# Linear attention and two MLPs on one core: sums of weight parts and low halves of W2's parts made by GpSimd in place of VectorE

## The chip, the cores and the metric

The kernel runs on one core of a Trainium2 chip. The metric is the time of one execution in microseconds on the device, as the median of several runs. A profile is one more execution, taken by the hardware profiler; its own time stands beside it. Engines are named PE (TensorE, matmuls), PEld (TensorE's weight loads), DVE (VectorE), ACT (ScalarE), POOL (GpSimd) and SP (SyncE, whose queue issues DMAs).

## The reference

```python
kv = np.einsum('bhsd,bhse->bhde', k, v)          # 4 x 8 heads, 576 tokens, 64 wide
out = np.einsum('bhsd,bhde->bhse', q, kv)
rms = np.sqrt(np.mean(out * out, axis=-1, keepdims=True) + 1e-06)
x = (out / rms * g_norm)                         # -> [2304, 512]
h = x @ moe_w_in                                 # [512, 2048]
g = np.maximum(h, 0.0) + np.log1p(np.exp(-np.abs(h)))
x = (g @ moe_w_out)                              # [2048, 512]
h = x @ moe2_w_in
g = np.maximum(0.01 * h, h)
return (g @ moe2_w_out)
```

The weights arrive as 64-bit floats.

## The kernel before

The attention takes the first 80 us. After it the activations lie in SBUF as `xy`, 512 features by 2304 tokens, and the two MLPs run over them in place. Each MLP is cut into four groups of 512 hidden columns (`NG` = 4, so groups 0 to 7), each group into three tiles of 768 tokens (`NTP`), each tile into two steps of 256 hidden columns.

A matmul in full precision is three matmuls here. An operand is split into a high half, which ScalarE makes by a copy to the narrower type fp32r, and a low half, the rest, which is one subtraction of VectorE with two inputs in SBUF; the products high by high, high by low and low by high are added in PSUM. Line 850 and line 855 do this for the hidden activations `g` (in `parts`), lines 739 and 734 for the inputs, lines 1003 and 1006 for W2's parts.

To save matmuls, most products of 2 x 2 blocks are made from seven products of sums of blocks in place of eight (`PROD` names the sums). So weights and activations are first added and subtracted blockwise. `split_pair` does that for W1: four sums in series of 128x256 (line 656), then the two halves of the seven parts (lines 673 and 677). It is called twice for each of the eight groups; for the first group with `first` set, during the attention. `w2_part` does it for W2 in the groups 1, 2, 5, 6 and 7 (`SG`): over its seven calls four sums of 128x512 (line 989) and for each part one high half (line 1003) and one low half (line 1006). Those seven calls stand in the last tile before such a group: this document calls that the entry into the group. Before both, `decode_w` turns 64-bit weights into 32-bit ones: a copy on ScalarE (line 595), then a shift (line 601) and two operations with two inputs in SBUF (lines 607 and 613) on VectorE.

What comes out of a step's products lies in PSUM banks. ScalarE copies some of it out (line 1119), VectorE adds the rest (line 1126), and the bank is free for a later product (line 821). The second layer's results are added to `xy` by VectorE from PSUM (lines 1050 and 711). In these two kinds of addition only one input lies in SBUF.

The order is made by `Plan`, when the program is built. Each piece of work is given by `op` with an engine or a choice of engines, a cost in microseconds (`t_d` for VectorE, `t_a` for ScalarE, `t_p` for GpSimd), what it reads and what it writes. `Plan.run` goes through time with one clock for each engine, takes for an engine that is free the ready piece with the earliest due time, and writes the instructions in that order into each engine's queue. The order is fixed then: an instruction that waits holds up all that stands behind it in its queue. The engines' clocks in the plan are independent of each other.

Of the kernel before, what the change touches and what calls it, by code (L numbers as in the profile page):

```python
# [19 lines left out]
class Plan:  # L20
# [18 lines left out]
    def op(self, cost, fn, reads=(), writes=(), due=None):  # L39
        o = {"cost": cost, "fn": fn, "succ": [], "n": len(self.ops)}  # L40
        deps = {}
        for k in reads:
            if k in self.writer:
                deps[self.writer[k]["n"]] = self.writer[k]
        for k in writes:
            for d in [self.writer.get(k), *self.readers.get(k, ())]:
                if d is not None:
                    deps[d["n"]] = d
        for k in reads:
            self.readers.setdefault(k, []).append(o)  # L50
        for k in writes:
            self.writer[k], self.readers[k] = o, []
        o["deps"] = list(deps.values())
        for d in o["deps"]:
            d["succ"].append(o)
        o["due"] = self.pe
        if "PE" in cost:
            self.pe += cost["PE"]
        else:
            o["due"] += self.AHEAD  # L60
        if due is not None:
            o["due"] = due
        self.ops.append(o)
        return o
# [67 lines left out]
def linear_attention_two_mlps(  # L132
# [32 lines left out]
    nc = tc.nc  # L165
    B, H, S, D = q.shape
    NT, DM = out.shape
    DFF = w1.shape[1] // 2
    P = 128
# [166 lines left out]
    op = plan.op  # L336
    ENG = {"D": nc.vector, "P": nc.gpsimd}

    def t_a(n):
        return 0.1 + n * 0.84e-3  # L340

    def t_d(n, fast=False):
        return 0.08 + n * (0.8e-3 if fast else 1.04e-3)

    def t_p(n):
        return 0.2 + n * 2.5e-3
# [301 lines left out]
    def part(r, j, n=1):  # L648
        return r.keys(1024 * j, 1024 * (j + n))

    def split_pair(i, u, first=False):
        r, w_ = sraw[i], wst[u]

        def combine(j, a, b, sign):
            def fn(e):
                ENG[e].tensor_tensor(r[:, j, :], r[:, a, :], r[:, b, :], sign)

            op({"D": t_d(256)}, fn, part(r, a) + part(r, b), part(r, j))

        def parts(j, at, n):  # L660
            hk = w_.keys(at * 1024, (at + n) * 1024)
            lk = w_.keys(7168 + at * 1024, 7168 + (at + n) * 1024)
            sk = part(r, j, n)
            m = n * 256

            def ends(a):
                return (
                    w_[:, a, at * 256:(at + n) * 256],
                    r.ap.rearrange("p a b -> p (a b)")[:, j * 256:(j + n) * 256],
                )  # L670

            def hi(e):
                nc.scalar.activation(*ends(0), AF.Copy)

            def lo(e):
                out, in_ = ends(1)
                ENG[e].tensor_tensor(out, in_, ends(0)[0].bitcast(F32), ALU.subtract)

            op({"A": t_a(m)}, hi, sk, hk)
            op({"D": t_d(m)}, lo, sk + hk, lk)  # L680


        if first:
            x_, hk = wx[u], wx[u].keys()
            op({"A": t_a(256)}, lambda e: nc.scalar.activation(x_[:, 0, :], r[:, 0, :], AF.Copy),
               part(r, 0), hk)
            op(
                {"D": t_d(256)},
                lambda e: nc.vector.tensor_tensor(
                    x_[:, 1, :], r[:, 0, :], x_[:, 0, :].bitcast(F32), ALU.subtract  # L690
                ), part(r, 0) + hk, hk,
            )
        parts(1, 0, 3)
        combine(1, 0, 1, ALU.add)
        combine(0, 2, 0, ALU.subtract)
        combine(2, 1, 2, ALU.subtract)
        combine(3, 3, 2, ALU.subtract)
        parts(0, 3, 4)
# [273 lines left out]
    def w2_part(g, i):  # L972


        def blk(a, u):
            at = (3 + 4 * u) * KI // 4
            ap = bufs["rc"][:, at:at + 2 * DM].rearrange("p (m f) -> p m f", m=2)
            return ap[:, :, a * 256:(a + 1) * 256]

        def bk(a, u):  # L980
            return [k_ for m in range(2) for k_ in fS[u][m].keys(1024 * a, 1024 * (a + 1))]

        r = [(lambda a=a, u=u: blk(a, u), bk(a, u)) for a in range(2) for u in range(2)]
        r.append((lambda: fT.ap, fT.keys()))

        def combine(to, x, y, sign):
            op(
                {"D": t_d(512)},
                lambda e: nc.vector.tensor_tensor(r[to][0](), r[x][0](), r[y][0](), sign),
                r[x][1] + r[y][1], r[to][1],  # L990
            )

        if i == 1:
            combine(4, 0, 1, ALU.add)
        elif i == 2:
            combine(0, 2, 0, ALU.subtract)
            combine(2, 4, 2, ALU.subtract)
        elif i == 3:
            combine(4, 3, 2, ALU.subtract)
        src, sk = r[(2, 4, 2, 4, 0, 3, 1)[i]]  # L1000
        w_ = wS[g // NG][PROD[i][2]]
        hk, lk = w_.keys(0, 2048), w_.keys(2048)
        op({"A": t_a(512)}, lambda e: nc.scalar.activation(w_[:, 0], src(), AF.Copy), sk, hk)  # L1003
        op(
            {"D": t_d(512)},
            lambda e: nc.vector.tensor_tensor(  # L1006
                w_[:, 1], src(), w_[:, 0].bitcast(F32), ALU.subtract
            ), sk + hk, lk,
        )
# [17 lines left out]
    def second(t):  # L1027
# [26 lines left out]
        def piece(i, j):  # L1054
# [48 lines left out]
            if t % NTP == NTP - 1 and g + 1 in SG:  # L1103
                w2_part(g + 1, i)
# [175 lines left out]
    for s in range(2 * NT2 + 2):  # L1280
# [11 lines left out]
        if enters:  # L1292
            g_held[0] = True
            for i in range(2):
                g_part(t, i)
                w2_part(t // NTP, i)
# [26 lines left out]
        if enters:  # L1323
            g_part(t, 3)
            for i in range(2, 7):
                w2_part(t // NTP, i)
# [62 lines left out]
```

## Time and profile before

| | us |
|---|---|
| median of 3 runs | 801.38 |
| the three runs | 800.7, 801.38, 802.01 |
| the profiled execution, whole | 800.57 |
| its span, first to last instruction | 798.5 |
| PE busy | 787.5 |
| DVE busy | 688.2 |
| ACT busy | 453.3 |
| POOL busy | 18.2 |

The span is what the profile's rows cover; 2.07 us of the profiled execution lie outside it. Matmuls follow each other in a pipeline, so PE's busy time tells that it had work, not that the array was full; how often PE waited, and for whom, is told by the view of waits. An idle time of another engine matters only where PE waits for that engine.

### The profile page before, as it was taken

Reading aid. Unit: us, or ns where it says so; the run is one execution under the profiler, and the core shown is the slowest. Engines: PE = TensorE matmul, PEld = TensorE weight load, DVE = VectorE, ACT = ScalarE, POOL = GpSimd, SP = SyncE. Lnnn points to the kernel's source line nnn. Section 1 sums busy time; section 2 is a strip of 40 time slices with the busy share of each in tenths; the row PEclk is TensorE's granted clock in tenths of the full one; section 3 lists DMA queues with packets and bytes.
Section 4 is the critical chain, followed back from the end, with each engine's and each line's share of the span. In section 5 each row is a group of like instructions: output and inputs, shape, how many; then the busy total and the mean of one; then the engine's idle time right before and its main releaser. Section 6 shows DMA issues by size and latency. Waiting matters only on the chain.

```text
span 798.5 us, 13018 instructions
## 1 busy us (share of the span) xinstructions
PE 787.5 (99%) x4962; PEld 774.9 (97%) x4962; DVE 688.2 (86%) x1129; ACT 453.3 (57%) x753; POOL 18.2 (2%) x35
## 2 busy tenths in 40 slices
PE   8899999999999999999999999999999999999997
PEld 7899999999999999999999988989999999999997
DVE  6989997989999999996698877868989999997776
ACT  5877965565465455563466566546456555554341
POOL 3320000000000000000000000000000000000000
PEclk9999999999999999999999999999999999999999
DMA  9990993675874675596776986874854764753914
GB/s 311 306 332 27 361 369 127 273 286 188 308 259 148 226 303 182 224 336 213 289 289 265 376 300 241 307 229 179 326 170 145 281 233 184 255 195 122 317 40 119
DMA packets 77294, 192.47 MB, mean 241 GB/s; under 512 B 11569, under 2 KB 50481, under 8 KB 77233
## 3 DMA queue, kind: packets, MB, share of 16 engines
q1 hardware_dynamic: 75344, 190.73, 66.4%
q10 hardware_dynamic: 1888, 0.92, 0.4%
q8 instruction: 39, 0.64, 0.3%
q14 instruction: 23, 0.18, 0.1%
HBM read 152.31 MB, written 39.32 MB: 240 GB/s over the span
## 4 chain that ended last, share of the span: by engine, by line
PE 97%; ACT 1%; DMA 1%; DVE 1%; SPq 0%; issue 0%; POOL 0%; ACTq 0%; POOLq 0%
PE ps L821 42%; PE ps L1072 17%; PE ps L1172 13%; PE ps L1077 11%; PE ps L1190 6%; PE ps L459 2%; PE ps L915 2%; PE ps L422 2%; PE ps L414 1%; PE ps L543 1%; DMA qa<-in_q_dram 1%; PE ps L465 0%; PE ps L425 0%; PE ps L555 0%; ACT xy L531 0%
## 5 line engine op out<-in xcount | busy, mean ns | idle before, releaser
L821 PE MATMUL ps<-ra 128*128 128x384 f32 x1932 | 387.4, 335 | 0.0
L821 PEld LDWEIGHTS ps<-ra 128*128 128x128 f32 x1932 | 334.9, 188 | 3.8
L850 ACT ACTIVATE rb<-mf 128x768 fp32r<-128x768 f32 x131 | 110.8, 846 | 91.9 <-PE ps L1072 43.9
L1072 PE MATMUL ps<-rb 128*128 128x256 f32 x1134 | 153.1, 281 | 0.0
L1072 PEld LDWEIGHTS ps<-rb 128*128 128x128 f32 x1134 | 148.7, 189 | 0.0
L855 DVE TENSOR_TENSOR rb<-mf,rb 128x768 fp32r<-128x768 f32 x131 | 124.6, 953 | 16.0 <-ACT rb L850 15.5
L1050 DVE TENSOR_TENSOR xy<-ps,xy 128x512 f32<-128x512 f32 (+2 forms) x213 | 116.3, 549 | 23.2 <-PE ps L1072 16.1
L1172 PE MATMUL ps<-rb 128*128 128x384 f32 x576 | 113.7, 334 | 0.0
L1172 PEld LDWEIGHTS ps<-rb 128*128 128x128 f32 x576 | 101.1, 188 | 0.0
L1077 PE MATMUL ps<-rb 128*128 128x384 f32 x504 | 100.8, 334 | 0.0
L1119 ACT ACTIVATE mf<-ps 128x384 f32<-128x384 f32 x118 | 57.8, 490 | 72.6 <-PE ps L821 69.8
L1126 DVE TENSOR_TENSOR mf<-ps,mf 128x384 f32<-128x384 f32 x118 | 65.4, 554 | 36.6 <-PE ps L821 35.1
L1077 PEld LDWEIGHTS ps<-rb 128*128 128x128 f32 x504 | 88.5, 188 | 0.0
L1190 PE MATMUL ps<-rb 128*128 128x512 f32 x216 | 56.8, 394 | 0.0
L836 ACT ACTIVATE mf<-mf 128x768 f32<-128x768 f32 (+1 forms) x44 | 29.9, 679 | 27.9 <-DVE mf L1126 27.9
L1190 PEld LDWEIGHTS ps<-rb 128*128 128x128 f32 x216 | 39.9, 188 | 5.7
L952 DVE TENSOR_TENSOR mf<-mf 128x768 f32<-128x768 f32 x40 | 38.1, 953 | 0.8 <-ACT mf L842 0.3
L842 ACT ACTIVATE mf<-mf 128x384 f32<-128x384 f32 (+1 forms) x42 | 27.6, 658 | 18.9 <-DVE mf L1126 18.5
L1006 DVE TENSOR_TENSOR rb<-rc,rb 128x512 fp32r<-128x512 f32 x35 | 23.8, 685 | 2.0 <-ACT rb L1003 2.0
L1003 ACT ACTIVATE rb<-rc 128x512 fp32r<-128x512 f32 x35 | 21.5, 626 | 5.7 <-PE ps L1190 2.4
L607 DVE SCALAR_TENSOR_TENSOR sqr<-mf,sqr 128x512 int32<-128x512 int32 x35 | 24.0, 685 | 0.3
L706 ACT ACTIVATE xy<-ps 128x512 f32<-128x512 f32 (+1 forms) x26 | 14.2, 548 | 14.6 <-PE ps L1172 11.6
(117 smaller groups left out, 775.3 us busy)
## 6 DMA issues: line engine op xcount, KB each, us to landing
ra<-xscr SPq DMA_DIRECT2D x131, 768.0 KB, 6.3
xscr<-ra SPq DMA_DIRECT2D x30, 768.0 KB, 6.3
mf<-in_moe_w_in_dram SPq DMA_DIRECT2D x18, 512.0 KB, 5.1
xscr<-rc SPq DMA_DIRECT2D x12, 768.0 KB, 3.9
mf<-in_moe_w_out_dram SPq DMA_DIRECT2D x17, 512.0 KB, 5.0
lf<-in_moe_w_out_dram SPq DMA_DIRECT2D x15, 512.0 KB, 4.3
lf<-in_moe_w_in_dram SPq DMA_DIRECT2D x14, 512.0 KB, 5.3
qa<-in_q_dram SPq DMA_DIRECT2D x16, 256.0 KB, 5.5
```

The source lines that it names most:

```text
L821: nc.tensor.matmul(o, w_[:, a, c:c + P], e_[:, b, kk, :], start=(not on and kk == 0 and n == 0), stop=(kk == 1 and n == 2), skip_group_che ...
L836: {"A": t_a(n)}, lambda e: nc.scalar.activation(dst(), src(), AF.Softplus),
L850: {"A": t_a(n)}, lambda e: nc.scalar.activation(g[:, 0, :, :], c.ap, AF.Copy),
L855: lambda e: nc.vector.tensor_tensor(g[:, 1, :, :], c.ap, g[:, 0, :, :].bitcast(F32), ALU.subtract),
L952: lambda e: nc.vector.tensor_tensor(to.ap, x.ap, y.ap, ALU.subtract),
L1050: {"D": t_d(n)}, lambda e: nc.vector.tensor_tensor(dst, src, dst, ALU.add),
L1072: nc.tensor.matmul(y[:, 256 * (j % 2):256 * (j % 2 + 1)], G_[:, a, m, js], w_[:, b, m, :], **flags)
L1077: nc.tensor.matmul(y[:, :BN], w_[:, a, m, js], G_[:, b, m, :], **flags)
L1119: {"A": t_a(BN)}, lambda e: nc.scalar.activation(c[:, m, :], src, AF.Copy),
L1126: lambda e: nc.vector.tensor_tensor(c[:, m, :], src, c[:, m, :], ALU.add),
L1172: nc.tensor.matmul(y[:, :BN], w_[m][:, a, js], G_[:, b, m, :], start=(u == 0 and m == 0 and i == 0), stop=(u == 1 and m == 1 and i == 2),)
L1190: nc.tensor.matmul(y, G_[:, a, m, js], w_[m][:, b, :], start=(u == 0 and m == 0 and i == 0), stop=(u == 1 and m == 1 and i == 2),)
```

## The change

Three kinds of work get GpSimd as their engine, with GpSimd's cost in the plan: the sums of W1 parts in `split_pair`, except those of the first group; the sums of W2 parts in `w2_part`; and the low halves of W2's seven parts there.

```diff
@@ -655,7 +655,7 @@
             def fn(e):
                 ENG[e].tensor_tensor(r[:, j, :], r[:, a, :], r[:, b, :], sign)
 
-            op({"D": t_d(256)}, fn, part(r, a) + part(r, b), part(r, j))
+            op({"D": t_d(256)} if first else {"P": t_p(256)}, fn, part(r, a) + part(r, b), part(r, j))
 
         def parts(j, at, n):
             hk = w_.keys(at * 1024, (at + n) * 1024)
@@ -985,8 +985,8 @@
 
         def combine(to, x, y, sign):
             op(
-                {"D": t_d(512)},
-                lambda e: nc.vector.tensor_tensor(r[to][0](), r[x][0](), r[y][0](), sign),
+                {"P": t_p(512)},
+                lambda e: nc.gpsimd.tensor_tensor(r[to][0](), r[x][0](), r[y][0](), sign),
                 r[x][1] + r[y][1], r[to][1],
             )
 
@@ -1002,8 +1002,8 @@
         hk, lk = w_.keys(0, 2048), w_.keys(2048)
         op({"A": t_a(512)}, lambda e: nc.scalar.activation(w_[:, 0], src(), AF.Copy), sk, hk)
         op(
-            {"D": t_d(512)},
-            lambda e: nc.vector.tensor_tensor(
+            {"P": t_p(512)},
+            lambda e: nc.gpsimd.tensor_tensor(
                 w_[:, 1], src(), w_[:, 0].bitcast(F32), ALU.subtract
             ), sk + hk, lk,
         )
```

In the plan `t_d(256)` is 0.35 us, `t_d(512)` 0.61, `t_p(256)` 0.84 and `t_p(512)` 1.48. The plan makes a new order from them. The order of PE's instructions is the same in both kernels. GpSimd's queue, which ended with the attention, gets 111 instructions behind it.

VectorE's queue at the entry into group 1, before, from the low half of an activation (line 855) to the second of the two additions from PSUM (line 1126; `ps_84` is the bank):

```order
L855 TENSOR_TENSOR rb<-mf,rb 128x768
L613 SCALAR_TENSOR_TENSOR rc<-rc,sqr 128x512
L952 TENSOR_TENSOR mf<-mf 128x768
L989 TENSOR_TENSOR rc<-rc 128x512
L989 TENSOR_TENSOR rc<-rc 128x2x256
L855 TENSOR_TENSOR rb<-mf,rb 128x768
L1006 TENSOR_TENSOR rb<-rc,rb 128x512
L1126 TENSOR_TENSOR mf<-ps_85,mf 128x384
L989 TENSOR_TENSOR rc<-rc 128x2x256
L989 TENSOR_TENSOR rc<-rc 128x512
L1006 TENSOR_TENSOR rb<-rc,rb 128x512 x2
L1126 TENSOR_TENSOR mf<-ps_84,mf 128x384
```

The same stretch of VectorE's queue now:

```order
L855 TENSOR_TENSOR rb<-mf,rb 128x768
L952 TENSOR_TENSOR mf<-mf 128x768
L855 TENSOR_TENSOR rb<-mf,rb 128x768
L601 TENSOR_SCALAR sqr<-lf 128x512
L1126 TENSOR_TENSOR mf<-ps_85,mf 128x384
L607 SCALAR_TENSOR_TENSOR sqr<-mf,sqr 128x512
L613 SCALAR_TENSOR_TENSOR lf<-lf,sqr 128x512
L601 TENSOR_SCALAR sqr<-lf 128x512
L607 SCALAR_TENSOR_TENSOR sqr<-lf,sqr 128x512
L1126 TENSOR_TENSOR mf<-ps_84,mf 128x384
```

Four sums and three low halves have left it, and five decode operations (lines 601, 607 and 613) that stood further back have taken their places.

GpSimd's queue now, from the end of the attention (line 360) through the entry into group 1 to the first sum of the entry into group 2:

```order
L360 TENSOR_SCALAR kp_121<-ka_102 128x512
L656 TENSOR_TENSOR lf<-lf 128x256 x4
L656 TENSOR_TENSOR mf<-mf 128x256 x4
L1006 TENSOR_TENSOR rb<-rc,rb 128x512
L989 TENSOR_TENSOR rc<-rc 128x512
L989 TENSOR_TENSOR rc<-rc 128x2x256
L1006 TENSOR_TENSOR rb<-rc,rb 128x512
L989 TENSOR_TENSOR rc<-rc 128x2x256
L989 TENSOR_TENSOR rc<-rc 128x512
L1006 TENSOR_TENSOR rb<-rc,rb 128x512 x5
L989 TENSOR_TENSOR rc<-rc 128x512
```

Before, its queue ended with the first of these rows; the others were VectorE's.

## Rows read from the trace of the kernel before

**Rows 1.** The page: busy times by engine, and the chain that ended last.
```profile
PE 787.5 (99%) x4962; PEld 774.9 (97%) x4962; DVE 688.2 (86%) x1129; ACT 453.3 (57%) x753; POOL 18.2 (2%) x35
...
PE 97%; ACT 1%; DMA 1%; DVE 1%; SPq 0%; issue 0%; POOL 0%; ACTq 0%; POOLq 0%
```

**Rows 2.** Waits of PE, first and last of seven: us in total, times, longest.
```profile
PE ps L1241 <- POOL ident masks.py:199: 2.0, 1, 2.0
...
PE ps L555 <- ACT xy L531: 0.3, 1, 0.3
```

**Rows 3.** Timeline of DVE, first sums that move: start, duration, line, operation, count.
```profile
133.47 1.80 DVE L656 TENSOR_TENSOR lf<-lf 128x256 f32<-128x256 f32 x4
```

**Rows 4.** The five entries: length, busy PE, PEld, DVE, ACT, POOL, granted clock, DMA.
```profile
161.90:183.90 22.00, 22.00 (x129) 22.00 (x128) 20.69 (x33) 14.57 (x27) 0.00 (x0) 1.00 0.85 312
251.20:272.50 21.30, 21.30 (x125) 21.30 (x124) 20.66 (x35) 13.24 (x24) 0.00 (x0) 1.00 0.73 259
485.80:545.20 59.40, 59.40 (x302) 53.66 (x301) 42.83 (x67) 34.45 (x58) 0.00 (x0) 1.00 0.71 252
614.80:633.80 19.00, 19.00 (x137) 19.00 (x137) 18.38 (x31) 11.34 (x19) 0.00 (x0) 1.00 0.80 284
704.30:723.40 19.10, 19.10 (x137) 19.10 (x136) 19.02 (x32) 11.97 (x20) 0.00 (x0) 1.00 0.81 287
```

**Rows 5.** DVE by line and shape: count, busy us, mean ns, idle before.
```profile
L855 DVE TENSOR_TENSOR rb<-mf,rb 128x768 fp32r<-128x768 f32 x131 | 124.6, 953 | 16.0 <-ACT rb L850 15.5
L1126 DVE TENSOR_TENSOR mf<-ps,mf 128x384 f32<-128x384 f32 x118 | 65.4, 554 | 36.6 <-PE ps L821 35.1 <-issue 0.3
...
L607 DVE SCALAR_TENSOR_TENSOR sqr<-mf,sqr 128x512 int32<-128x512 int32 x35 | 24.0, 685 | 0.3
L1006 DVE TENSOR_TENSOR rb<-rc,rb 128x512 fp32r<-128x512 f32 x35 | 23.8, 685 | 2.0 <-ACT rb L1003 2.0
...
L656 DVE TENSOR_TENSOR mf<-mf 128x256 f32<-128x256 f32 x36 | 15.3, 424 | 0.8
...
L601 DVE TENSOR_SCALAR sqr<-mf 128x512 int32<-128x512 int32 x22 | 9.3, 421 | 4.9 <-ACT mf L595 4.5
...
L510 DVE SCALAR_TENSOR_TENSOR fm<-fm,fa 128x20 f32<-128x20 f32 x8 | 1.8, 221 | 0.3
```

**Rows 6.** Timeline of DVE, the last low halves that move.
```profile
722.09 1.29 DVE L1006 TENSOR_TENSOR rb<-rc,rb 128x512 fp32r<-128x512 f32 x2
```

**Rows 7.** Timeline of POOL and DVE in the attention, two meetings.
```profile
15.23 1.23 DVE L677 TENSOR_TENSOR ra<-mf,ra 128x1024 fp32r<-128x1024 f32 x1
...
15.90 1.03 POOL L360 TENSOR_SCALAR kp<-ka 128x512 f32<-128x512 f32 x1 [1.41 <-DMA ka<-in_k_dram]
...
27.00 0.62 POOL L360 TENSOR_SCALAR qp<-qa 128x512 f32<-128x512 f32 x1 [1.00 <-DMA qa<-in_q_dram]
...
27.12 0.52 DVE L510 SCALAR_TENSOR_TENSOR fm<-fm,fa 128x20 f32<-128x20 f32 x1
```

**Rows 8.** Timeline of DVE at the entry into group 1.
```profile
165.76 0.95 DVE L855 TENSOR_TENSOR rb<-mf,rb 128x768 fp32r<-128x768 f32 x1
166.63 0.69 DVE L613 SCALAR_TENSOR_TENSOR rc<-rc,sqr 128x512 int32<-128x512 int32 x1
...
168.10 1.41 DVE L989 TENSOR_TENSOR rc<-rc 128x512 f32<-128x512 f32 x2
...
170.30 0.69 DVE L1006 TENSOR_TENSOR rb<-rc,rb 128x512 fp32r<-128x512 f32 x1
...
171.49 1.41 DVE L989 TENSOR_TENSOR rc<-rc 128x512 f32<-128x512 f32 x2
173.81 1.29 DVE L1006 TENSOR_TENSOR rb<-rc,rb 128x512 fp32r<-128x512 f32 x2 [0.91 <-ACT rb L1003]
175.02 0.55 DVE L1126 TENSOR_TENSOR mf<-ps,mf 128x384 f32<-128x384 f32 x1
```

**Rows 9.** Timeline of PE, the product that takes up the freed bank.
```profile
177.05 1.20 PE L821 MATMUL ps<-ra 128*128 128x384 f32 x6
```

## The prediction

> **What bounds the kernel now.** I began with the page's busy times and its chain: TensorE is busy 787.5 us of a span of 798.5 us, and 97% of the chain that ended last is TensorE's own work [rows 1]. The second view is who TensorE waited for. It has seven rows that sum to 6.5 us, and all of them are lines of the warm-up and the attention, its transposes and small matmuls [rows 2]; the attention is over before 80 us. The first sum that the change moves stands at 133.47 us [rows 3]. From there to the end TensorE waits for nobody: in the five stretches in which W2's parts are made it is busy for the whole of each, at a granted clock of 1.00, its upper level of 2.4 GHz [rows 4]. So the time is the attention's start plus an unbroken run of matmuls, in an order that the change leaves as it was. Nothing on VectorE can shorten that run; it can only be broken. The question is whether VectorE, 19.02 us busy of 19.10 in the tightest of these stretches [rows 4], comes late for TensorE after the change.
>
> **What is removed.** 56 of the 64 sums of W1 parts leave VectorE (the first pair's eight stay) and all 20 sums and 35 low halves of W2 parts: 56 x 0.423 + 55 x 0.685 = 61.4 us of VectorE [rows 5]. I count that as worth nothing: it is cover, not path. A gain is excluded for the same reason, since none of TensorE's seven waits lies behind the first moved instruction. Behind the last matmul too nothing changes: the last moved low halves stand at 722.09 us [rows 6], 76 us ahead of the end.
>
> **What is added.** GpSimd gets 111 subtractions and additions with two inputs in SBUF. It has none in this trace; the nearest row is its copy of 128x512 with one input, 0.62 us where nothing is in its way [rows 7]. If the second input were free, a W2 operation would take 0.62 us; if the inputs are read one behind the other, twice that, 1.24 us; with the write as a third pass, 0.14 + 3 x 0.48 = 1.58 us, where 0.48 us is the part that works on the data, read off just below, and 0.14 us the start. I take 1.24 us: two inputs and one engine that took 0.62 us for one. The Trainium skill (GPSIMD Engine Reference, section 3.1) gives 4497 ns for such an addition of 2048 columns; a quarter is 1.12 us, an estimate, by which the sum below would come to 805.4 us in place of 807.8.
>
> **The port.** Rows 7 show what the two engines do to each other. At 15.90 us GpSimd's copy meets a VectorE subtraction with two SBUF inputs that runs from 15.23 to 16.46: it takes 1.03 us in place of 0.62 and ends at 16.93, 0.47 us behind VectorE's end. At 27.00 us it is the other way about: GpSimd runs from 27.00 to 27.62, and VectorE's small operation on two SBUF tensors, line 510, which starts at 27.12, takes 0.52 us, against a mean of 221 ns over its line [rows 5], and ends at 27.64, with GpSimd. So an operation of VectorE with two SBUF inputs and one of GpSimd don't run side by side: whoever has begun keeps the other out. From the first meeting a GpSimd operation needs about 0.48 us of its 0.62 alone. A W2 operation of 1.24 us would then keep VectorE's two-input work out for 1.1 us. What was 0.685 us on VectorE becomes up to 1.1 us of VectorE standing still. The Trainium skill says the same in its page SBUF — State Buffer (section "SBUF: two separate sides"): VectorE's second port is GpSimd's only one, an exclusive lock for a whole instruction. The trace agrees, with the two meetings above; without such a lock the change would cost nothing.
>
> **Where it breaks.** The planner counts GpSimd as free beside VectorE and fills VectorE's emptied places with other work. The first entry into a group with W2 parts shows it, from the low half at 165.76 us to the addition of line 1126 that ends at 175.57 us, 9.81 us [rows 8]. In the changed order the same two ends have other rows between them. Gone are four sums (2 x 1.41 us), three low halves (0.69 and 1.29), and line 613 of 0.69, which now stands earlier; idle in it were 0.91 us. That leaves 9.81 - 0.91 - 2.82 - 1.98 - 0.69 = 3.4 us. Come in have five decode rows (lines 601, 607, 613, 601, 607), 2 x 0.421 + 3 x 0.685 = 2.9 us [rows 5]. VectorE's own work is 6.3 us. Seven GpSimd operations belong to the same stretch. If each meets a two-input operation, they add 7 x 1.1 = 7.7 us: 14.0 us, 4.2 later than before. If two of the seven fall beside the additions from PSUM or the shifts, it is 5 x 1.1 = 5.5: 11.8 us, 2.0 later. TensorE takes up the bank that this addition frees at 177.05 us [rows 9], a lead of 1.48 us. So TensorE stands still for 0.5 to 2.7 us there; I take the middle, 1.6.
>
> There are five such entries. In four of them VectorE has 0.1 to 1.3 us of idle time in some 20 us; in the one at 485.8 us it has 16.6 us, and that one I count at nothing [rows 4]. The sum is 4 x 1.6 = 6.4 us. The W1 sums come in 14 rows of four: 4 holds of about 0.55 us (half a W2 hold) in place of 4 x 0.42, a slip of 0.5 us, under the lead of 1.48 us: nothing, and 14 x 0.5 = 7 us if that lead is used up already. What is queued behind GpSimd's results: ScalarE's copies of line 1003 to the high halves and, on VectorE, line 677. Ahead of them in the order stands what the planner reckons GpSimd to need, 1.48 and 0.84 us, over my prices, so they wait only as far as the port makes GpSimd late.
>
> The profiled execution took 800.57 us (span 798.5 and 2.07 around it): 800.57 + 6.4 = 807.0. It lies 0.81 us under the median of the runs, 801.38, so the forecast is **807.8 us**, 0.8% slower.
>
> **The rivals.** First, **no change**. It decides at the number of meetings: 9.81 + 1.48 - 6.3 = 5.0 us is room for four holds of 1.1 us of the seven. If the operations mostly fall beside work that reads PSUM, where the trace shows 0.62 us and no delay, each entry stays under the lead. Time 801.4 us, within about 0.6. For it speaks that 61.4 us leave VectorE; against it that of the ten rows that VectorE keeps in the stretch worked out six have two SBUF inputs and two are shifts, of which no row shows whether they meet GpSimd.
>
> Second, **a dearer GpSimd**. At 1.58 us a hold is 1.44 us: 7 holds give 5.1 us an entry, 5 give 2.2, in the middle 3.65, four entries 14.6 us: 816 us, at most 821.8. The sums then also come late for ScalarE, whose copies from PSUM stand behind line 1003, and the W1 rows begin to tell. For it speaks that no row shows a two-input operation on GpSimd; against it that its one-input copies are steady at 0.62.
>
> Third, **faster**: only if something in the 76 us behind 722 us or in the attention moves, and the order shows no moved row there.
>
> **How the numbers follow.** The forecast gets 0.58, the dearer GpSimd 0.21, no change 0.18, faster 0.03. A measurement of this kernel can tell 0.2%, 1.6 us, from nothing. The forecast at its low end, 4 x 0.5 = 2.0 us, is still slower by more than that, so slower has 0.58 + 0.21 + a little of the second case's edge, 0.80, the same 0.17 and faster 0.03. The range runs from 801.3 us, in the middle of the no-change case, to 818 us, inside the dearer case: some 0.12 lie below and 0.07 above.
>
> **What would show it.** Right: GpSimd's operations of 128x512 at 1.1 to 1.3 us when alone and well over that when they meet VectorE; VectorE's two-input rows with means over 953 and 685 ns, its rows from PSUM at 554 ns as before; TensorE with waits for VectorE's lines 1126 and 1050, in the stretches behind the entries at 162, 251, 615 and 704 us, and few at 486 us. Wrong: TensorE still without waits behind 80 us (no change), or waits at every row of W1 sums (dearer). It would also be wrong if TensorE waited for GpSimd's results themselves rather than for VectorE.

## The result, and the profile after

The changed kernel takes 809.34 us (median of 5 runs, 809.25 to 809.38) against 801.38 us before (5 runs, 800.7 to 802.01): a ratio of 1.0097, 95% interval 1.0086 to 1.0109. It is 8.0 us slower; the two profiled executions lie 8.8 us apart. The forecast was 807.8 us, the range 801.3 to 818.

The page of the profile after, its busy times and the chain that ended last:

```profile
span 807.6 us, 13090 instructions
...
PE 789.4 (98%) x4962; PEld 774.2 (96%) x4962; DVE 668.2 (83%) x1016; ACT 451.5 (56%) x755; POOL 165.4 (20%) x146
...
PE 83%; DVE 12%; ACT 2%; issue 1%; POOL 1%; DMA 0%; ACTq 0%; DVEq 0%
```

TensorE's share of the chain, 97% before [rows 1], is 83%, and VectorE has 12%. VectorE's busy time fell from 688.2 to 668.2 us, by 20 us, though 61.4 us of work left it: some 41 us came back in the work that stayed. GpSimd's grew by 147 us.

Who TensorE waited for (us in total, times, longest); eleven rows, of which the first three and the last stand here:

```profile
PE ps L821 <- DVE mf L1126: 2.9, 3, 1.1
PE ps L1072 <- DVE xy L1050: 2.6, 2, 1.8
PE ps L1241 <- POOL ident masks.py:199: 2.0, 1, 2.0
...
PE ps L555 <- ACT xy L531: 0.3, 1, 0.3
```

The first two rows are new; in [rows 2] nothing of the MLPs waited. All five waits are for VectorE's additions from PSUM, lines 1126 and 1050. No row of the MLPs names GpSimd: TensorE never waited for its results directly. The other nine rows belong to the warm-up and the attention.

Some of VectorE's and GpSimd's costliest groups after (line, engine, operation, shape, count, then busy us, mean ns, idle before):

```profile
L855 DVE TENSOR_TENSOR rb<-mf,rb 128x768 fp32r<-128x768 f32 x131 | 133.7, 1020 | 24.6 <-ACT rb L850 23.9
L1126 DVE TENSOR_TENSOR mf<-ps,mf 128x384 f32<-128x384 f32 x118 | 65.2, 552 | 37.2 <-PE ps L821 36.6
...
L607 DVE SCALAR_TENSOR_TENSOR sqr<-mf,sqr 128x512 int32<-128x512 int32 x35 | 26.5, 757 | 0.6
...
L601 DVE TENSOR_SCALAR sqr<-mf 128x512 int32<-128x512 int32 x22 | 11.0, 501 | 6.0 <-ACT mf L595 5.6
```

```profile
L1006 POOL TENSOR_TENSOR rb<-rc,rb 128x512 fp32r<-128x512 f32 x35 | 54.8, 1568 | 131.3 <-ACT rb L1003 131.3
...
L989 POOL TENSOR_TENSOR rc<-rc 128x512 f32<-128x512 f32 x20 | 33.8, 1692 | 95.5 <-DVE rc L613 94.4
L656 POOL TENSOR_TENSOR mf<-mf 128x256 f32<-128x256 f32 x28 | 29.5, 1055 | 74.1 <-DVE ra L677 72.4
```

Beside [rows 5], the same forms with two SBUF inputs have grown, 953 to 1020 ns and 685 to 757, the shift of line 601 too, 421 to 501; the addition from PSUM has not, 554 to 552. On GpSimd the shortest of the 128x512 operations take 1.28 to 1.30 us and the shortest of the 128x256 ones 0.73 to 0.74; the means are 0.27 to 0.4 us over that.

The entry into group 1, the stretch of [rows 8], on VectorE, then on GpSimd (start us, duration, operation):

```profile
165.70 0.95 DVE L855 TENSOR_TENSOR rb<-mf,rb 128x768 fp32r<-128x768 f32 x1
166.68 1.93 DVE L952 TENSOR_TENSOR mf<-mf 128x768 f32<-128x768 f32 x1
169.53 1.05 DVE L855 TENSOR_TENSOR rb<-mf,rb 128x768 fp32r<-128x768 f32 x1 [0.92 <-ACT rb L850]
170.80 1.22 DVE L601 TENSOR_SCALAR sqr<-lf 128x512 int32<-128x512 int32 x1 [0.22 <-ACT lf L595]
171.94 0.54 DVE L1126 TENSOR_TENSOR mf<-ps,mf 128x384 f32<-128x384 f32 x1
172.41 1.31 DVE L607 SCALAR_TENSOR_TENSOR sqr<-mf,sqr 128x512 int32<-128x512 int32 x1
173.75 1.66 DVE L613 SCALAR_TENSOR_TENSOR lf<-lf,sqr 128x512 int32<-128x512 int32 x1
175.51 1.33 DVE L601 TENSOR_SCALAR sqr<-lf 128x512 int32<-128x512 int32 x1
176.87 1.66 DVE L607 SCALAR_TENSOR_TENSOR sqr<-lf,sqr 128x512 int32<-128x512 int32 x1
178.46 0.55 DVE L1126 TENSOR_TENSOR mf<-ps,mf 128x384 f32<-128x384 f32 x1
```

```profile
165.86 3.91 POOL L989 TENSOR_TENSOR rc<-rc 128x512 f32<-128x512 f32 x2 [4.78 <-DVE rc L613]
169.73 2.00 POOL L1006 TENSOR_TENSOR rb<-rc,rb 128x512 fp32r<-128x512 f32 x1
171.69 3.17 POOL L989 TENSOR_TENSOR rc<-rc 128x512 f32<-128x512 f32 x2
174.82 4.86 POOL L1006 TENSOR_TENSOR rb<-rc,rb 128x512 fp32r<-128x512 f32 x3
```

The two engines take turns. Line 952 starts at 166.68 us and takes 1.93 us in place of 0.95, because the first sum of GpSimd, which had itself waited behind line 855, runs first; the operations that follow, a low half, two sums and two low halves, do the same to lines 601, 607, 613, 601 and 607. Together with 0.10 us on the second line 855 that is 5.4 us over the means of [rows 5]. The two additions of line 1126 among them run at their 0.55 us. The second one ends at 179.01, and TensorE, which would have gone on at once, stands still:

```profile
176.80 1.20 PE L1172 MATMUL ps<-rb 128*128 128x384 f32 x6
179.06 1.33 PE L821 MATMUL ps<-ra 128*128 128x384 f32 x6 [1.06 <-DVE mf L1126]
```

The dearest place is the entry into group 6. TensorE before, at and after its longest wait:

```profile
636.48 1.21 PE L821 MATMUL ps<-ra 128*128 128x384 f32 x6
639.53 0.98 PE L1072 MATMUL ps<-rb 128*128 128x256 f32 x6 [1.84 <-DVE xy L1050]
640.34 2.02 PE L821 MATMUL ps<-ra 128*128 128x384 f32 x6
```

Six matmuls of line 821 span 1.21 us ahead of the wait and 2.02 us behind it. The view by windows (length, busy times of PE, PEld, DVE, ACT, POOL, granted clock, DMA) tells why:

```profile
636.00:639.00 3.00, 1.69 (x12) 1.36 (x10) 3.00 (x5) 3.00 (x6) 1.19 (x1) 1.00 0.94 340
640.50:644.30 3.80, 3.80 (x17) 3.80 (x16) 3.00 (x6) 0.49 (x1) 0.00 (x0) 0.56 0.41 138
644.30:648.00 3.70, 3.70 (x29) 3.70 (x28) 3.13 (x6) 1.91 (x3) 0.00 (x0) 1.00 0.43 142
```

The window from 640.50 in the kernel before:

```profile
640.50:644.30 3.80, 3.80 (x28) 3.80 (x28) 3.73 (x6) 2.40 (x4) 0.00 (x0) 1.00 0.42 142
```

Behind the wait the granted clock is 0.56 in the mean over 3.8 us, the lower of the two levels (1.2 GHz) for 3.4 us of it, and 17 matmuls get done where the kernel before does 28 in the same window. Half of 3.4 us, 1.7 us, is lost to the clock.

What made VectorE late here are holds again. From 624 to 638 us four of its operations take 3.0 us more than their means, each beside a low half of GpSimd (these start at 623.56, 625.57, 631.22 and 635.89 us):

```profile
624.47 0.93 DVE L601 TENSOR_SCALAR sqr<-mf 128x512 int32<-128x512 int32 x1
...
626.37 1.45 DVE L613 SCALAR_TENSOR_TENSOR mf<-mf,sqr 128x512 int32<-128x512 int32 x1
...
631.33 2.04 DVE L855 TENSOR_TENSOR rb<-mf,rb 128x768 fp32r<-128x768 f32 x1
...
636.43 1.57 DVE L952 TENSOR_TENSOR rc<-mf,rc 128x768 f32<-128x768 f32 x1
```

### The profile page after: what moved, and what is told of

It reads as the page before. It is cut to its first block, busy times and chain, and to the rows that moved or that the text cites. A ratio compares the mean times of both kernels' runs of the same rounds, so it can differ in the third digit from the quotient of the medians.

```text
span 807.6 us, 13090 instructions
## 1 busy us (share of the span) xinstructions
PE 789.4 (98%) x4962; PEld 774.2 (96%) x4962; DVE 668.2 (83%) x1016; ACT 451.5 (56%) x755; POOL 165.4 (20%) x146
## 4 chain that ended last, share of the span: by engine, by line
PE 83%; DVE 12%; ACT 2%; issue 1%; POOL 1%; DMA 0%; ACTq 0%; DVEq 0%
PE ps L821 36%; PE ps L1072 14%; PE ps L1172 12%; PE ps L1077 8%; PE ps L1190 6%; DVE rb L855 3%; PE ps L459 2%; DVE xy L1050 2%; PE ps L915 2%; DVE mf L952 1%; DVE sqr L607 1%; PE ps L422 1%; DVE sqr L601 1%; DVE ra L677 1%; DVE mf L1126 1%
## 5 line engine op out<-in xcount | busy, mean ns | idle before, releaser
L855 DVE TENSOR_TENSOR rb<-mf,rb 128x768 fp32r<-128x768 f32 x131 | 133.7, 1020 | 24.6 <-ACT rb L850 23.9
L1006 POOL TENSOR_TENSOR rb<-rc,rb 128x512 fp32r<-128x512 f32 x35 | 54.8, 1568 | 131.3 <-ACT rb L1003 131.3
L656 POOL TENSOR_TENSOR lf<-lf 128x256 f32<-128x256 f32 x28 | 28.2, 1008 | 224.7 <-DVE ra L677 223.1
L989 POOL TENSOR_TENSOR rc<-rc 128x512 f32<-128x512 f32 x20 | 33.8, 1692 | 95.5 <-DVE rc L613 94.4
L656 POOL TENSOR_TENSOR mf<-mf 128x256 f32<-128x256 f32 x28 | 29.5, 1055 | 74.1 <-DVE ra L677 72.4
L952 DVE TENSOR_TENSOR mf<-mf 128x768 f32<-128x768 f32 x40 | 42.7, 1068 | 2.1 <-ACT mf L842 1.2
```

The source lines that it names most:

```text
L855: lambda e: nc.vector.tensor_tensor(g[:, 1, :, :], c.ap, g[:, 0, :, :].bitcast(F32), ALU.subtract),
L1006: lambda e: nc.gpsimd.tensor_tensor(w_[:, 1], src(), w_[:, 0].bitcast(F32), ALU.subtract), sk + hk, lk,
```

## The experiments

Three theories stood against each other. Port: GpSimd, while it reads SBUF, keeps out VectorE's operations with two SBUF inputs, and VectorE comes late for TensorE. Data: GpSimd is slower, and its results come late. Order: the planner's new order costs the time by itself. Each ratio below is to the kernel before, timed with it (801.26 or 801.22 us).

**Fills in place of sums.** The whole change, in the same order, but GpSimd's operations work on 4 columns (two times 4 in W2's sums and halves) and then fill their whole output twice with a constant, which leaves out the sums and low halves:

```diff
+    def mostly_set(out, x, y, sign):
+        few = (slice(None), slice(None), slice(0, 4)) if len(out.shape) == 3 else (slice(None), slice(0, 4))
+        nc.gpsimd.tensor_tensor(out[few], x[few], y[few], sign)
+        for _ in range(2):
+            nc.gpsimd.memset(out.bitcast(F32) if out.dtype != F32 else out, 0.01)
...
-                lambda e: nc.gpsimd.tensor_tensor(r[to][0](), r[x][0](), r[y][0](), sign),
+                lambda e: mostly_set(r[to][0](), r[x][0](), r[y][0](), sign),
```

> The change in whole, but each moved operation on GpSimd works on its first 4 columns alone (so that it still waits for its inputs) and then fills its output twice with a constant, an operation that only writes SBUF; the sums and low halves are left out, so the output is not the reference's. From rows: a fill of 512 columns takes 0.52 us, two in a row 0.99, so a W2 operation takes about 1.2 us in place of 1.29 without company. Port theory (GpSimd's reading of SBUF keeps VectorE's operations with two SBUF inputs waiting, VectorE comes late for TensorE): line 855 back to 953 ns, lines 607 and 613 to 685, no wait of TensorE behind 90 us, time 800.7 to 802.5 us. Data theory (GpSimd is slower than VectorE, its results come late for ScalarE and through it for TensorE): nearly the same length of work on GpSimd, so most of the 8 us stay, 806 to 809 us. Order theory (the planner's new order alone costs the time): the order is the same as the changed kernel's, 809 us.

Measured: 801.69 us, ratio to the kernel before 1.0004 (0.9994 to 1.0015). GpSimd was busy for 155.7 us, nearly as long as the 165.4 of the changed kernel. VectorE's two-input rows went back to their old means (line 855 has become 860):

```profile
PE 788.4 (99%) x4962; PEld 775.6 (97%) x4962; DVE 637.9 (80%) x1016; ACT 455.0 (57%) x755; POOL 155.7 (19%) x368
...
L860 DVE TENSOR_TENSOR rb<-mf,rb 128x768 fp32r<-128x768 f32 x131 | 125.0, 954 | 28.7 <-ACT rb L855 28.3
L607 DVE SCALAR_TENSOR_TENSOR sqr<-mf,sqr 128x512 int32<-128x512 int32 x35 | 24.0, 687 | 0.6
```

TensorE had no wait in the MLPs. So neither the order, which is the same, nor the length of GpSimd's work costs anything there; its reading of SBUF does. Data and order are out as the cause of the 8 us. One limit: a fill waits for less than a sum does, since only the few columns in front of it tie it to its inputs. The stretch at the entry into group 1 speaks against such waits as the cause: VectorE idles there for 1.1 us, for ScalarE, and 0.9 us before [rows 8], while its lengthened operations make 5.4 us.

**The old order.** The same operations on GpSimd, but reckoned as VectorE's, so that every queue keeps its old order:

```diff
-                lambda e: nc.vector.tensor_tensor(r[to][0](), r[x][0](), r[y][0](), sign),
+                lambda e: nc.gpsimd.tensor_tensor(r[to][0](), r[x][0](), r[y][0](), sign),
```

(the same for the low halves and for the W1 sums, each with its `{"D": ...}` kept).

> The same 111 operations on GpSimd, but the planner still reckons them as VectorE's, with VectorE's costs: the order of every queue is that of the kernel before, with the 111 taken out of VectorE's queue and put on GpSimd's, and nothing filled into the places. Port theory: VectorE is held as often (some 30 to 40 us in all) but has 61 us less work in the same stretches and nothing new in them, so its slips are smaller: 802.5 to 806 us. Data theory: the planner now leaves 0.61 and 0.35 us for operations that take 1.29 and 0.74, so results come later than in the changed kernel: over 809 us, with waits that go back to GpSimd. Order theory: 801.4 us.

Measured: 804.58 us, ratio 1.0042 (1.0028 to 1.0056), inside what the port theory gave. Without new work in the freed places VectorE slips less, and less than half of the loss is left. Of TensorE's three waits of over 0.1 us in the MLPs two are for VectorE's additions from PSUM (1.15 and 0.51 us). The third is the data theory's, at 140 us: GpSimd's four W1 sums, then ScalarE, then TensorE (timeline):

```profile
134.26 4.55 POOL L659 TENSOR_TENSOR lf<-lf 128x256 f32<-128x256 f32 x4 [73.43 <-DVE ra L680]
```

```profile
138.84 1.06 ACT L676 ACTIVATE ra<-lf 128x1024 fp32r<-128x1024 f32 x1 [2.78 <-POOL lf L659]
139.80 0.47 ACT L1122 ACTIVATE mf<-ps 128x384 f32<-128x384 f32 x1
```

```profile
140.33 0.96 PE L824 MATMUL ps<-ra 128*128 128x384 f32 x4 [0.85 <-ACT mf L1122]
```

The planner had left 0.35 us for each sum, which takes 1.14 us here; ScalarE stands 2.78 us before line 676, and its copy out of PSUM behind it comes 0.85 us late for TensorE. So late results do cost time where the order leaves none for them, about 1.0 us of this kernel's 3.3; the changed kernel's order, with 0.84 us a sum, leaves it.

**A planner that knows of the port.** The whole change, with one more clock in the plan:

```diff
+        def ready(o, e):
+            return max(o["at"][e], port) if o["port"] else o["at"][e]
...
-                t = max(t, o["at"][e])
+                t = max(t, ready(o, e))
...
+                if o["port"]:
+                    port = o["end"]
```

and `port=True` on GpSimd's operations and on VectorE's with two SBUF inputs and the shift.

> The change in whole, with the same costs, but the planner knows of the port: an operation of GpSimd or of VectorE with two SBUF inputs (and the shift of line 601) may not be placed beside another such one. Port theory: the planner puts VectorE's additions from PSUM beside GpSimd's work and keeps the due times, 800.7 to 802.5 us, with GpSimd's rows nearer to 1.29 and 0.74 us. Data theory: GpSimd's operations take as long and start later, so no better than 809. Order theory: a third order, about which it has nothing to say but that 801.4 would be chance.

Measured: 800.62 us, ratio 0.999 (0.9981 to 1.0). The loss is gone, with the same 111 operations on GpSimd at the same price in the plan, and TensorE has no wait over 0.1 us in the MLPs. But one thing expected did not come: the engines still meet.

The groups that were lines 855 and 1006:

```profile
L861 DVE TENSOR_TENSOR rb<-mf,rb 128x768 fp32r<-128x768 f32 x131 | 130.7, 1002 | 17.2 <-ACT rb L856 16.8
```

```profile
L1012 POOL TENSOR_TENSOR rb<-rc,rb 128x512 fp32r<-128x512 f32 x35 | 53.1, 1523 | 115.4 <-ACT rb L1009 114.3 <-PE ps L1078 1.1
```

1002 and 1523 ns are hardly under the 1020 and 1568 of the changed kernel. The order didn't avoid the meetings; it left time for them, so that the additions from PSUM stand where they are in time after the meetings.

**The parts alone.** The low halves of W2 alone, the W1 sums alone, the W2 sums alone; each takes its own lines of the diff.

> Of the change only the 35 low halves of W2's parts; all sums stay on VectorE. Port theory: 35 holds of 1.1 us in the five entries in place of 55, and most of the waits are at the entries at 162 and 615 us: 804 to 807 us. Data theory: what the low halves feed is TensorE directly, so TensorE waits for GpSimd's line 1006: some waits of that name, 803 to 805. Order theory: another order, 801.4 to 809.

> Of the change only the 56 sums of W1 parts. The prediction counted them at nothing: a row of four on GpSimd slips VectorE by some 0.5 us, under TensorE's lead of 1.5 us. Port theory: 800.7 to 802.5 us, though GpSimd's rows meet VectorE's and read about 1.0 us in place of 0.74. The other possibility that the prediction named, a lead that is used up already: 14 rows by 0.5 us, 808 us. Data theory: VectorE's and ScalarE's lines 677 and 673 wait for GpSimd, as the changed kernel's rows show with 16 us in nine waits; if that reached TensorE, 803 us or more.

> Of the change only the 20 sums of W2 parts. Four holds of about 1.1 us in each entry, under the room for four that the prediction worked out (5.0 us): port theory 800.7 to 802.5 us. If the losses of the parts simply added up (the whole change 8.0 us, the low halves alone 5.8), the W1 sums and W2 sums would bring 2.2 us between them: 802 to 803.5 for one of them.

Measured: the low halves 807.02 us, ratio 1.0069 (1.0054 to 1.0084); the W1 sums 800.92, 0.9993 (0.9984 to 1.0002); the W2 sums 800.82, 0.9995 (0.9983 to 1.0006). For the low halves the wait by name that the data theory asked for, on line 1006, is not there; TensorE waits for lines 1050 and 1126:

```profile
PE ps L1072 <- DVE xy L1050: 1.9, 1, 1.9
PE ps L821 <- DVE mf L1126: 1.7, 2, 1.4
```

The low halves have the half clock too, from 639 to 642 us:

```profile
639.00:642.00 3.00, 3.00 (x13) 3.00 (x13) 1.97 (x3) 0.49 (x1) 0.00 (x0) 0.50 0.19 62
```

The parts don't add up: 0 + 0 + 5.8 us against 8.0. Sums alone slip VectorE too (a row of four W1 sums has means of over 1.0 us on GpSimd), but stay under TensorE's lead.

**Without the worst entry.** The whole change except in group 6, in the sums and in the low halves of W2's parts alike:

```diff
-                {"P": t_p(512)},
+                {"D": t_d(512)} if g == 6 else {"P": t_p(512)},
```

> The whole change except in the group that is entered at 615 us in the kernel before, whose W2 sums and low halves stay on VectorE. The changed kernel's trace shows at that entry waits of TensorE of 1.0, 1.2 and 2.0 us at 577, 634 and 640 us, and 3.4 us at half the granted clock behind the last. Port theory: all of that goes, 6 us, and the rest stays: 802.5 to 804.5 us, with no stretch at half clock. If the slip were not tied to the place but to the amount of GpSimd work (55 operations of 128x512, 11 fewer), a fifth of the loss goes: 807 to 808 us.

Measured: 803.84 us, ratio 1.0028 (1.0015 to 1.004). 5.5 us of the 8.0 go with one entry of five. The waits at 179 and 268 us stay, with 1.08 and 0.75 us; those from 577 to 640 us and the half clock are gone (by windows, columns as above):

```profile
570.00:585.00 15.00, 15.00 (x109) 15.00 (x108) 12.09 (x19) 6.20 (x10) 0.00 (x0) 1.00 0.67 274
620.00:650.00 30.00, 30.00 (x216) 30.00 (x215) 28.97 (x47) 16.41 (x28) 0.00 (x0) 1.00 0.63 220
```

A wait of 0.47 us at 694.74 is new: the order behind has moved as well.

**The port in the plan once more**, in 11 executions.

> The whole change with the planner that knows of the port once more, in more rounds, to tell whether it is faster than the kernel before. It stood at 0.999, interval 0.9981 to 1.0. Port theory: TensorE has no wait behind 90 us in either kernel, so there is nothing to be gained: within 0.1% of the kernel before.

Measured: 800.89 us, ratio 0.9993 (0.9984 to 1.0002). It is as fast as the kernel before, not faster. No version here beats that kernel: TensorE has no wait left behind 90 us that VectorE's relief could take away.

## Why the prediction was right, point by point

**The bound.** TensorE's unbroken run could only be broken, and it was: relieving VectorE gave nothing in any of the runs, not even where 61.4 us left it and no meeting cost TensorE anything (fills in place of sums, 801.69 us).

**The port.** Read off two meetings in the attention [rows 7], it was the cause. The fills settle it: same order, same engine, nearly the same busy time, next to no reading, no loss.

**The price on GpSimd.** Taken as 1.24 us, measured 1.28 to 1.30 us alone; for 128x256 I went by half a W2 operation, which is 0.62, and it is 0.73 to 0.74. The Trainium skill's figure (GPSIMD Engine Reference, section 3.1) gave 1.12 as an estimate for 512 columns, by which the sum was put at 805.4 us (with a hold of 0.98 us in place of 1.1 it is nearer 805.1). The measurement is above both prices. The dearer case, 1.58, is out.

**The entry worked out.** For group 1 I had VectorE's stretch at 11.8 to 14.0 us and TensorE's wait at 0.5 to 2.7, taken as 1.6. They are 13.3 us (165.70 to 179.01) and 1.06 us of wait, about 1.3 with TensorE's start behind it. That the length fits is in part luck. VectorE's own work came to 6.8 us, not 6.3; it waited 1.1 us for ScalarE (lines 850 and 595), which I had at nothing; and the seven operations of GpSimd cost 5.4 us, under the lowest case, 5.5, since the six that counted held VectorE for 0.6 to 1.0 us each and not for 1.1. The lead was larger than [rows 9] say: TensorE could have gone on at about 177.84 us, 12.1 us behind the start of VectorE's stretch in place of 11.3.

**Four equal entries.** This is the step that was off. I took 4 x 1.6 = 6.4 us. From one matmul's start to the next, beyond their normal distance, TensorE lost about 1.3 us at the entry into group 1, 1.1 at group 2, 0 at group 5 as counted, 6.1 at group 6 and 0.3 at group 7, 8.8 in all. Group 6 has three waits, of 0.81, 1.05 and 1.84 us (1.0, 1.2 and 2.0 from start to start). The first, at 577 us, comes from two sums that the planner had put some 40 us ahead of the entry's low halves, in a place that the stretches of [rows 4] don't cover; and the third brings the half clock. Idle time of VectorE in a stretch [rows 4] does not tell these entries apart: group 7 had the least, 0.1 us, and lost nearly nothing.

**The clock.** 1.7 of the 8.8 us were not in the sum at all. No row of the MLPs before shows a clock under 1.00.

**The terms taken as nothing.** The W1 sums alone and the W2 sums alone cost nothing, as counted; the room for four holds held for four sums. In the whole change the sums, with the order that comes with them, add to the low halves: 8.0 against 5.8 us. The wait at 577 us stands behind two W2 sums; how the rest divides between the two kinds of sums no run tells.

**The rivals.** No change would have needed at most four meetings of seven; at the entry into group 1 there were six that cost 0.6 us or more. Results that come late for TensorE did not show in the changed kernel, and did in the one with the old order. That the forecast lies 1.5 us under the result is an error of two that go opposite ways: three entries cost less than taken, and one cost more and lost the clock.

## What to carry to other kernels

Moving work off a busy engine pays only where another engine waits for it, and it can cost where the two share a way into SBUF: of the 61.4 us taken off VectorE some 41 came back, since its operations with two SBUF inputs stand still while GpSimd reads. If such work must go there, the order has to count the shared port as an engine of its own; then the same move cost nothing. And a wait can cost more than itself: behind the two longest of the MLPs, of 1.84 and 1.9 us, TensorE ran at the lower clock for 3.4 us.

## What the runs showed of the hardware

The shift of line 601, one input from SBUF and its output there, is kept out by GpSimd even when GpSimd only writes. With fills on GpSimd, on VectorE at the same entry:

```profile
171.58 0.79 DVE L601 TENSOR_SCALAR sqr<-lf 128x512 int32<-128x512 int32 x1 [0.44 <-ACT lf L595]
...
173.04 0.68 DVE L607 SCALAR_TENSOR_TENSOR sqr<-mf,sqr 128x512 int32<-128x512 int32 x1
```

and on GpSimd:

```profile
171.56 1.27 POOL L981 MEMSET rc<- 128x512 f32 x2
...
173.18 1.11 POOL L981 MEMSET rc<- 128x512 f32 x2
```

The shift takes 0.79 us in place of 0.42 beside a fill; line 607 with its two inputs runs beside the next fills in its usual 0.68. The Trainium skill (SBUF — State Buffer, section "Who interferes with whom") says that a VectorE operation with two SBUF inputs contends with GpSimd operations that read and not with those that only write, and VectorE's two-port modes with GpSimd's whatever they do. Line 607 agrees with the first; the shift fits the second if it runs in such a mode, which no row here tells.

In the MLPs the granted clock fell behind a wait of 1.84 us that began 4 us after the end of one of 1.05, and in the kernel with the low halves alone behind one of 1.9 us that began 4 us after the end of one of 0.3; it did not fall behind the other waits, of 0.5 to 1.4 us. What of the length and the nearness of waits decides, these runs don't tell.
